# Retention in four chunks of 112 tokens and one of 128, where there were four of 128 and one of 64

## The chip, the cores and the metric

The kernel runs on one core of a Trainium2 chip. The metric is the device time of one execution in microseconds: 867.72 before the change, the median of three runs (867.5 to 868.18). A core has TensorE (PE, with its weight loads as PEld), VectorE (DVE), ScalarE (ACT), GpSimd (POOL) and SyncE (SP, which here only issues DMAs).

## The reference

Causal retention over 4 batches, 8 heads, 576 tokens and head dimension 64, and then two feed-forward layers over the 2304 x 512 result:

```python
scores = scale * np.matmul(q, k.transpose(0, 1, 3, 2))      # scale = 1/8
gamma = 1.0 - 2.0 ** (-5.0 - np.arange(H))
Dmat = np.where(rel >= 0, gamma[:, None, None] ** rel, 0.0)  # rel = row - column
ret = np.matmul(scores * Dmat, v)                            # 4 x 8 x 576 x 64
x = ret.transpose(0, 2, 1, 3).reshape(2304, 512)
h = x @ w_in;  x = np.maximum(0.01 * h, h) @ w_out           # 512 -> 2048 -> 512
h = x @ w2_in; out = (h - np.tanh(h)) @ w2_out
```

The weights of the layers arrive as 64-bit floats.

## The kernel before, in words

Retention is computed by chunks. For a chunk of tokens, the near part is the masked score matrix of the chunk with itself, times v. The far part is q, scaled by powers of gamma, times a state of 64 x 64 that sums k times v over all chunks before. Two heads make a pair, and there are 16 pairs (`order`). The first 64 partitions hold one head's dimensions and the other 64 the other's, so that two products of 64 rows (or with an output of 64 rows) lie side by side in the array. 576 tokens are four chunks of 128 (`MAIN` = 512) and a tail of 64.

One pair `i` goes through these steps. Each engine works through its own instructions in the order in which they are written:

- `load` (two pairs ahead, on SP): transposed q and k of the pair, and k and v by tokens. The v by tokens has a fifth chunk: the last 128 tokens.
- `prep_k` (ACT, L613): k by tokens times gamma to the power of minus the row, for the states. `prep_tail` (ACT, L621; for the first pair DVE, L623): copies the last 64 columns of q, not yet scaled, into a block-diagonal tile `bd`, whose other half was set to zero once.
- `scores` (PE, L632): for each chunk and head one product of 64 rows, 128 x 128. The two heads go to the two banks of `sc`.
- `prep_q` (POOL, L602 and L607): q times its powers of gamma in place, first the 512 columns, then the 64.
- `mask` (DVE, L646): scores times mask and decay table `cm_sb`, one instruction a head, into `pt`.
- `pair_steps`: for pairs from 5 on first `unit_h` (PE, L758) and `unit_o` (PE, L783), which are products of the first layer for tokens that are done. Then the outputs of pair `i - 1`: `outputs_far` (L697) for chunks 1 to 3 and `outputs_near` (L708) for chunks 0 to 3 into the bank `o`, and both again for the tail into `x_t`. Then for pair `i` `states_mm` (L665, into the bank `x_c`) and `scores_tail` (L638): one product over the whole array, of k of the last 128 tokens with `bd`, into `x_a`. `states` (L673 on ACT, three L675 on DVE) adds up the states. `finish` (L716, L717) writes the output of pair `i - 1` as a rounded part and a rest, the tail first. `mask_tail` (DVE, L655) masks the last scores on the late 64 partitions; the early 64 of that part of `pt` were set to zero once. At the end stand `prep_tail` and `prep_k` of pair `i + 1`.

`x_a` and `x_t` are parts of one bank, `x_e`. Waits between engines on PSUM are by bank: a reader of a bank waits for the writes to that bank that were written before it in the program, and the other way round.

Between these steps `fill` sets the work that turns weights into two-part operands: 64-bit words are loaded (L149), narrowed to 32 bits (ACT L166, DVE L172, L177, L183 twice) and split (ACT L255, POOL L256). `marks` says how many of these operations stand in which third of which pair; the first eight weight pieces are used in the units, the others are kept in DRAM for later. SP's order is that of the program. A `load` of pair `i + 2` waits for the buffer of pair `i - 1`.

An fp32 product shows as two matmul instructions. So "x16" of L632 is eight products.

After the stage, `layers` (L275, L309, L428 and their helpers) does the rest; the change does not touch it. Columns, rows and parts that the steps touch are in the listing.

Of the kernel before, what the change touches and what calls it, by code (L numbers as in the profile page):

```python
# [10 lines left out]
F32 = mybir.dt.float32  # L11
# [3 lines left out]
AF = mybir.ActivationFunctionType  # L15
ALU = mybir.AluOpType
PSUM = bass.MemoryType.PSUM

P = 128
CH = 128  # L20

# [14 lines left out]
def retention_moe_moe(  # L36
# [16 lines left out]
    nc = tc.nc  # L53
    B, NP, _, S = qT.shape
    NT, DM = out.shape
    NF = w1i.shape[0]
    KK = DM // P
    NFULL = S // CH
    TAIL = S - NFULL * CH
    NCH = NFULL + 1  # L60
    MAIN = NFULL * CH
    LATE = CH - TAIL
    GF = 4
# [491 lines left out]
    def retention():  # L555
        with ExitStack() as ac:
            ak = ac.enter_context(tc.tile_pool(name="ak", bufs=1))
            ap_ = ac.enter_context(tc.tile_pool(name="ap", bufs=3))
            cw_pool[0] = ac.enter_context(tc.tile_pool(name="c0", bufs=2))
            ps_s = ac.enter_context(tc.tile_pool(name="ps_s", bufs=1, space=PSUM))  # L560
            ps_a = ac.enter_context(tc.tile_pool(name="ps_a0", bufs=1, space=PSUM))

            x_e = ps_s.tile([P, 3, TAIL], F32, name="x_e")
            x_a, x_t = x_e[:, :2, :], x_e[:, 2, :]
            x_b = ps_s.tile([P, 2, QW], F32, name="x_b")
            x_c = ps_s.tile([P, 512], F32, name="x_c")
            c_ = x_c[:, :NFULL * 64].rearrange("p (c d) -> p c d", d=64)


            cm_sb = ak.tile([P, NP, 2, CH], F32, name="cm_sb")  # L570
            qt_sb = ak.tile([P, NP, CH], F32, name="qt_sb")
            kt_sb = ak.tile([P, NP, 2], F32, name="kt_sb")
            sts = [ak.tile([P, NFULL, 64], F32, name=f"st{i}") for i in range(2)]
            decay = ak.tile([P, NP], F32, name="decay")
            pt_ = [ak.tile([P, 2, S], F32, name=f"pt{i}") for i in range(2)]
            bds = [ak.tile([P, 2, TAIL], F32, name=f"bd{i}") for i in range(2)]
            qk, kv, pts = {}, {}, {}
            order = [(b, p) for b in range(B) for p in range(NP)]

            def load(i):  # L580
                load_qk(i)
                load_v(i)

            def load_qk(i):
# [4 lines left out]
                qk[i] = t  # L589

            def load_v(i):
                b, p = order[i]
                t = ap_.tile([P, NFULL + NCH, P], F32, tag="kv", name="kv")
                nc.sync.dma_start(out=t[:, :NFULL, :], in_=kn[b, p])
                nc.sync.dma_start(out=t[:, NFULL:, :], in_=vn[b, p])
                kv[i] = t

            def prep_q(i):

                b, p = order[i]  # L600
                q = qk[i][:, 1, :MAIN].rearrange("p (c r) -> p c r", r=CH)
                nc.gpsimd.tensor_tensor(  # L602
                    out=q, in0=q, in1=qt_sb[:, p:p + 1, :].to_broadcast([P, NFULL, CH]),
                    op=ALU.mult,
                )
                q = qk[i][:, 1, MAIN:]
                nc.gpsimd.tensor_tensor(out=q, in0=q, in1=qt_sb[:, p, :TAIL], op=ALU.mult)  # L607

            def prep_k(i):
                b, p = order[i]  # L610
                for h in range(2):
                    k = kv[i][:, :NFULL, 64 * h:64 * h + 64]
                    nc.scalar.activation(out=k, in_=k, func=AF.Copy, scale=kt_sb[:, p, h:h + 1])  # L613

            def prep_tail(i):

                q = qk[i][:, 1, MAIN:]
                for h in range(2):
                    o = slice(64 * h, 64 * h + 64)
                    if i:  # L620
                        nc.scalar.activation(out=bds[i % 2][o, h, :], in_=q[o], func=AF.Copy)  # L621
                    else:
                        nc.vector.tensor_copy(out=bds[i % 2][o, h, :], in_=q[o])  # L623

            def scores(i):
                kt, qt = qk[i][:, 0, :], qk[i][:, 1, :]
                sc = ps_s.tile([P, 2, 512], F32, tag="sc", name="sc")
                for c in range(NFULL):
                    cs = slice(c * CH, (c + 1) * CH)
                    for h in range(2):  # L630
                        r = slice(64 * h, 64 * h + 64)
                        nc.tensor.matmul(  # L632
                            out=sc[:, h, cs], lhsT=kt[r, cs], rhs=qt[r, cs], start=True, stop=True
                        )
                return sc

            def scores_tail(i):
                nc.tensor.matmul(  # L638
                    out=x_a, lhsT=qk[i][:, 0, S - CH:], rhs=bds[i % 2], start=True, stop=True
                )  # L640

            def mask(i, sc):
                b, p = order[i]
                pt = pt_[i % 2]
                for h in range(2):
                    nc.vector.tensor_tensor(  # L646
                        out=pt[:, h, :MAIN].rearrange("p (c r) -> p c r", r=CH),
                        in0=sc[:, h, :].rearrange("p (c r) -> p c r", r=CH),
                        in1=cm_sb[:, p, h:h + 1, :].to_broadcast([P, NFULL, CH]), op=ALU.mult,
                    )  # L650
                pts[i] = pt

            def mask_tail(i):
                b, p = order[i]
                nc.vector.tensor_tensor(  # L655
                    out=pts[i][LATE:, :, MAIN:], in0=x_a[LATE:], in1=cm_sb[LATE:, p, :, LATE:],
                    op=ALU.mult,
                )

            def states_mm(i):  # L660
                t = kv[i]
                for c in range(NFULL):
                    for h in range(2):
                        o = slice(64 * h, 64 * h + 64)
                        nc.tensor.matmul(  # L665
                            out=c_[o, c, :], lhsT=t[:, c, o], rhs=t[:, NFULL + c, o],
                            start=True, stop=True,
                        )
# [11 lines left out]
            def chunk_out(o_, c):  # L680
                n = min(CH, S - c * CH)
                cs = slice(c * CH, c * CH + n)
                return (o_[:, cs] if c < NFULL else x_t), cs
# [6 lines left out]
            def outputs_far(i, o_, chunks):  # L690

                q, st = qk[i][:, 1, :], sts[i % 2]
                for c in chunks:
                    dst, cs = chunk_out(o_, c)
                    for h in range(2):
                        o = slice(64 * h, 64 * h + 64)
                        nc.tensor.matmul(  # L697
                            out=dst[o], lhsT=st[o, c - 1, :], rhs=q[o, cs],
                            start=c in (1, NFULL), stop=False, skip_group_check=True,
                        )  # L700

            def outputs_near(i, o_, chunks):
                pt, t = pts[i], kv[i]
                for c in chunks:
                    dst, cs = chunk_out(o_, c)
                    for h in range(2):
                        o = slice(64 * h, 64 * h + 64)
                        nc.tensor.matmul(  # L708
                            out=dst[o], lhsT=t[:, NFULL + c, o], rhs=pt[:, h, cs],
                            start=False, stop=True, skip_group_check=True,  # L710
                        )
# [93 lines left out]
            def pair_steps(i, fast):  # L805
# [26 lines left out]
                if i + 1 < len(order):  # L832
                    prep_tail(i + 1)
                    prep_k(i + 1)

            t = ap_.tile([P, 2, S], F32, tag="qk", name="qk")
# [276 lines left out]
```

## Time and profile before

| | |
|---|---|
| median of 3 runs | 867.72 us |
| the profiled execution | 868.1 us, its span 866.1 us |
| mean granted TensorE clock | 0.998 |
| PE busy | 850.1 us (98%), 5728 instructions |
| DVE busy | 604.1 us (70%) |
| ACT busy | 451.2 us (52%) |
| POOL busy | 377.1 us (44%) |
| DMA | 134.43 MB, mean 155 GB/s |

The span is from the first to the last instruction; the device time holds 2.0 us more around it. Busy shares are means over stages with different limits. The chain of waits goes back from the last instruction, at each step to what released it. A line of it is a stretch of time on one engine. Matmuls are pipelined and their ends are modelled, so the start of the next line says more than the duration of one matmul.

### The profile page before, as it was taken

What the parts mean: (1) busy time and instruction counts of PE and PEld (TensorE: products, weight loads), DVE (VectorE), ACT (ScalarE), POOL (GpSimd) and SP (SyncE); (2) the same over time, 40 slices, a digit from 0 to 9 for tenths busy, and PEclk for the clock granted to TensorE, in tenths of its full rate; (3) what the DMA queues carried; (4) which work ended last, traced back from release to release, by engine and by line L of the source; (5) the groups of instructions that cost most, each with busy time, mean ns of one, the idle gap of its engine ahead of it and who ended that gap; (6) DMA issues with size and microseconds to landing.
All of it is one profiled execution on the core that took longest, in us unless ns stands there. A gap on an engine that the chain in (4) does not pass through costs nothing.

```text
span 866.1 us, 15237 instructions
## 1 busy us (share of the span) xinstructions
PE 850.1 (98%) x5728; PEld 748.2 (86%) x5728; DVE 604.1 (70%) x1038; ACT 451.2 (52%) x899; POOL 377.1 (44%) x304
## 2 busy tenths in 40 slices
PE   6999999999999999999999999999999999999997
PEld 5889999888888889888888898888999899999996
DVE  5995767587786676658765577756676667777675
ACT  4553444453255433454444577666556566566663
POOL 2541222040036302464365379655545445545553
PEclk9999999999999999999999999999999999999999
DMA  9835663433454533644444503572225412563112
GB/s 340 315 125 172 219 209 118 150 121 103 135 213 186 179 121 110 243 170 127 190 175 165 195 1 146 226 284 75 75 96 180 162 73 74 208 231 121 49 50 74
DMA packets 38778, 134.43 MB, mean 155 GB/s; under 512 B 4400, under 2 KB 5936, under 8 KB 36656
## 3 DMA queue, kind: packets, MB, share of 16 engines
q1 hardware_dynamic: 38272, 133.25, 43.7%
q8 instruction: 45, 0.74, 0.4%
q14 instruction: 29, 0.24, 0.1%
q10 hardware_dynamic: 432, 0.20, 0.1%
HBM read 97.26 MB, written 36.18 MB: 154 GB/s over the span
## 4 chain that ended last, share of the span: by engine, by line
PE 89%; DVE 4%; DMA 2%; issue 2%; POOL 1%; ACT 1%; POOLq 0%; ACTq 0%; SPq 0%; DVEq 0%
PE a L428 40%; PE h L275 22%; PE h L309 17%; PE a L783 3%; PE x_b L758 3%; PE o L708 1%; PE sc L632 1%; PE o L697 1%; DVE cw L183 1%; DMA acc<-in_w1i 1%; DMA cm_sb<-in_cmask 1%; DVE pt L646 1%; PE x_c L665 0%; DVE v L394 0%; DMA kt_sb<-in_ktab 0%
## 5 line engine op out<-in xcount | busy, mean ns | idle before, releaser
L428 PE MATMUL a<-w 128*128 128x512 f32 (+1 forms) x1680 | 395.2, 377 | 0.5 <-POOL w L400 0.5
L428 PEld LDWEIGHTS a<-w 128*128 128x128 f32 x1680 | 293.1, 188 | 48.9 <-POOL w L400 1.3
L256 POOL TENSOR_TENSOR w<-cw,w 128x512 fp32r<-128x512 f32 x80 | 113.5, 1436 | 233.6 <-ACT w L255 207.8
L275 PE MATMUL h<-xh,w 128*128 128x512 f32 (+1 forms) x672 | 187.1, 349 | 0.0
L368 POOL TENSOR_TENSOR v<-t,u 128x512 f32<-128x512 f32 (+1 forms) x76 | 93.1, 1225 | 100.5 <-ACT t L365 96.4
L275 PEld LDWEIGHTS h<-xh,w 128*128 128x128 f32 x672 | 119.5, 188 | 17.0
L400 POOL TENSOR_TENSOR w<-v,w 128x512 fp32r<-128x512 f32 (+1 forms) x76 | 96.1, 1265 | 63.9 <-ACT w L399 63.9
L354 ACT ACTIVATE w<-h 128x512 fp32r<-128x512 f32 (+1 forms) x68 | 37.2, 547 | 160.3 <-PE h L275 115.4
L275 PE MATMUL h<-xl,w 128*128 128x512 f32 (+1 forms) x336 | 117.0, 348 | 0.0
L309 PE MATMUL h<-xh,w 128*128 128x256 f32 x512 | 100.9, 281 | 0.2
L309 PEld LDWEIGHTS h<-xe,w 128*128 128x128 f32 x576 | 80.8, 189 | 10.7 <-DVE mk L303 3.1
L183 DVE SCALAR_TENSOR_TENSOR cw<-st,cw 128x512 uint32<-128x512 uint32 x96 | 86.4, 900 | 2.5
L394 DVE SCALAR_TENSOR_TENSOR v<-q,v 128x512 f32<-128x512 f32 (+1 forms) x76 | 60.8, 800 | 37.1 <-POOL v L368 37.1
L364 ACT ACTIVATE u<-h 128x512 f32<-128x512 f32 (+1 forms) x80 | 44.2, 553 | 80.4 <-DVE h L303 53.2
L309 PEld LDWEIGHTS h<-xh,w 128*128 128x128 f32 x512 | 83.1, 190 | 2.8 <-DVE v L397 1.5
L309 PE MATMUL h<-xe,w 128*128 128x256 f32 x576 | 84.3, 282 | 1.1 <-DVE mk L303 1.0
L505 DVE TENSOR_TENSOR acc<-a,acc 128x512 f32<-128x512 f32 (+1 forms) x114 | 72.1, 657 | 18.5 <-PE a L428 18.5
L399 ACT ACTIVATE w<-v 128x512 fp32r<-128x512 f32 (+1 forms) x76 | 45.3, 596 | 61.5 <-DVE v L397 59.0
L172 DVE TENSOR_SCALAR cw<-cw 128x512 f32<-128x512 f32 x64 | 33.1, 518 | 57.7 <-ACT cw L166 57.6
L309 PE MATMUL h<-xl,w 128*128 128x256 f32 x256 | 71.8, 281 | 0.0
L275 PEld LDWEIGHTS h<-xl,w 128*128 128x128 f32 x336 | 63.3, 188 | 8.6
L383 DVE TENSOR_TENSOR h<-h,t 128x512 f32<-128x512 f32 (+1 forms) x80 | 51.3, 641 | 15.2 <-ACT t L365 15.2
(82 smaller groups left out, 1159.8 us busy)
## 6 DMA issues: line engine op xcount, KB each, us to landing
kept<-w SPq DMA_DIRECT2D x48, 512.0 KB, 3.5
w<-kept SPq DMA_DIRECT2D x48, 512.0 KB, 4.8
xe<-xkept SPq DMA_DIRECT2D x12, 1536.0 KB, 6.7
st<-in_w2i SPq DMA_DIRECT2D x16, 512.0 KB, 3.5
st<-in_w1i SPq DMA_DIRECT2D x12, 512.0 KB, 4.1
st<-in_w1o SPq DMA_DIRECT2D x12, 512.0 KB, 3.5
xkept<-xe SPq DMA_DIRECT2D x4, 1536.0 KB, 6.7
kv<-in_vn SPq DMA_DIRECT2D x16, 320.0 KB, 5.2
```

The costliest lines, as they stand in the source:

```text
L183: nc.vector.scalar_tensor_tensor(out=t["w"], in0=t[src], scalar=scalar, in1=t["w"], op0=op, op1=ALU.bitwise_or)
L256: nc.gpsimd.tensor_tensor(out=wp[:, 1, :], in0=wf, in1=wp[:, 0, :].bitcast(F32), op=ALU.subtract)
L275: nc.tensor.matmul(out=ps[:, :n], lhsT=w[:, wi, cs], rhs=x[:, kk, t0:t0 + n], start=kk == 0 and i == 0, stop=kk == KK - 1 and i == 2,)
L309: nc.tensor.matmul(out=out_, lhsT=w[:, wi_, at:at + P], rhs=x(xi, kk), start=start and kk == 0 and j == 0, stop=stop and kk == 1 and j == ...
L364: nc.scalar.activation(out=u[:, :n], in_=h, func=AF.Square)
L368: nc.gpsimd.tensor_tensor(out=v[:, :n], in0=t_[:, :n], in1=u[:, :n], op=ALU.mult)
L383: nc.vector.tensor_tensor(out=h, in0=h, in1=tmp[s][1][:, :n], op=ALU.subtract)
L394: nc.vector.scalar_tensor_tensor(out=v, in0=q, scalar=RHO_A, in1=v, op0=ALU.add, op1=ALU.mult)
L399: nc.scalar.activation(out=gt[:, 0, g_at(s)], in_=v, func=AF.Copy)
L400: (nc.gpsimd if m else nc.vector).tensor_tensor(out=gt[:, 1, g_at(s)], in0=v, in1=gt[:, 0, g_at(s)].bitcast(F32), op=ALU.subtract)
L428: nc.tensor.matmul(out=o, lhsT=l, rhs=r, start=f == 0 and i == 0 and d % pack == 0, stop=f == GF - 1 and i == 2 and (d + 1) % pack == 0, s ...
L505: nc.vector.tensor_tensor(out=dst, in0=a, in1=dst, op=ALU.add)
```

## The change

The chunks are now four of 112 tokens (`MAIN` = 448) and a last one of 128. `chunks_of` gives both numbers. The last chunk's v is no longer a fifth chunk of the v by tokens; it lies behind k in the tile `qk` and comes with k's load (for the first pair by a DMA of its own, after its other four). The products, masks and tables of the chunks take 112 rows and columns, those of the last chunk 128.

The last scores are one product of 64 rows a head, straight from q, into two banks. The copies of q (`bd`) and the two constant zero areas go. As the last scores now read q itself, the scaling of its last 128 columns on POOL stands behind them in `pair_steps`. `x_e` has two banks: one holds the last scores of the first head and `x_t`, the other those of the second head and the states `c_`, which had the bank `x_c`.

```diff
-CH = 128
+def chunks_of(S):
+    n = -(-S // P) - 1
+    return n, (S - P) // n
...
-            x_e = ps_s.tile([P, 3, TAIL], F32, name="x_e")
-            x_a, x_t = x_e[:, :2, :], x_e[:, 2, :]
+            x_e = ps_s.tile([P, 2, 512], F32, name="x_e")
+            x_a, x_t = x_e[:, :, :P], x_e[:, 0, P:2 * P]
             x_b = ps_s.tile([P, 2, QW], F32, name="x_b")
-            x_c = ps_s.tile([P, 512], F32, name="x_c")
-            c_ = x_c[:, :NFULL * 64].rearrange("p (c d) -> p c d", d=64)
+            c_ = x_e[:, 1, P:P + NFULL * 64].rearrange("p (c d) -> p c d", d=64)
...
-            bds = [ak.tile([P, 2, TAIL], F32, name=f"bd{i}") for i in range(2)]
...
+            def qk_tile():
+                return ap_.tile([P, 2 * S + P], F32, tag="qk", name="qk")
...
+            def v_of(i, c, o):
+                if c < NFULL:
+                    return kv[i][:CH, NFULL + c, o]
+                return qk[i][:, 2 * S:][:, o]
...
-                nc.sync.dma_start(out=t[:, 1, :], in_=qT[b, p])
-                nc.sync.dma_start(out=t[:, 0, :], in_=kT[b, p])
+                nc.sync.dma_start(out=t[:, :S], in_=qT[b, p])
+                nc.sync.dma_start(out=t[:, S:], in_=kT[b, p])
...
-                t = ap_.tile([P, NFULL + NCH, P], F32, tag="kv", name="kv")
-                nc.sync.dma_start(out=t[:, :NFULL, :], in_=kn[b, p])
-                nc.sync.dma_start(out=t[:, NFULL:, :], in_=vn[b, p])
+                t = ap_.tile([P, 2 * NFULL, P], F32, tag="kv", name="kv")
+                nc.sync.dma_start(out=t[:CH, :NFULL, :], in_=kn[b, p])
+                nc.sync.dma_start(out=t[:CH, NFULL:, :], in_=vn[b, p])
...
-                q = qk[i][:, 1, MAIN:]
-                nc.gpsimd.tensor_tensor(out=q, in0=q, in1=qt_sb[:, p, :TAIL], op=ALU.mult)
+
+            def prep_tail(i):
+                b, p = order[i]
+                q = q_of(i, MAIN)
+                nc.gpsimd.tensor_tensor(out=q, in0=q, in1=qt_sb[:, p, :], op=ALU.mult)
...
-            def prep_tail(i):
-
-                q = qk[i][:, 1, MAIN:]
-                for h in range(2):
-                    o = slice(64 * h, 64 * h + 64)
-                    if i:
-                        nc.scalar.activation(out=bds[i % 2][o, h, :], in_=q[o], func=AF.Copy)
-                    else:
-                        nc.vector.tensor_copy(out=bds[i % 2][o, h, :], in_=q[o])
...
             def scores_tail(i):
-                nc.tensor.matmul(
-                    out=x_a, lhsT=qk[i][:, 0, S - CH:], rhs=bds[i % 2], start=True, stop=True
-                )
+                for h in range(2):
+                    r = slice(64 * h, 64 * h + 64)
+                    nc.tensor.matmul(
+                        out=x_a[:, h, :], lhsT=k_of(i, MAIN)[r], rhs=q_of(i, MAIN)[r],
+                        start=True, stop=True,
+                    )
...
-                    out=pts[i][LATE:, :, MAIN:], in0=x_a[LATE:], in1=cm_sb[LATE:, p, :, LATE:],
-                    op=ALU.mult,
+                    out=pts[i][:, :, MAIN:], in0=x_a, in1=cm_sb[:, p], op=ALU.mult,
...
                     states_mm(i)
                     scores_tail(i)
+                    prep_tail(i)
                     states(i)
...
                 if i + 1 < len(order):
-                    prep_tail(i + 1)
                     prep_k(i + 1)
 
-            t = ap_.tile([P, 2, S], F32, tag="qk", name="qk")
-            nc.sync.dma_start(out=t[:, 1, :], in_=qT[0, 0])
+            t = qk[0] = qk_tile()
+            nc.sync.dma_start(out=t[:, :S], in_=qT[0, 0])
             nc.scalar.dma_start(out=cm_sb[:, 0], in_=cmask[:, 0])
-            nc.sync.dma_start(out=t[:, 0, :], in_=kT[0, 0])
-            qk[0] = t
+            nc.sync.dma_start(out=t[:, S:2 * S], in_=kT[0, 0, :, :S])
             nc.scalar.dma_start(out=kt_sb, in_=ktab)
             nc.scalar.dma_start(out=qt_sb[:, 0, :], in_=qtab[:, 0, :])
             load_v(0)
+            nc.sync.dma_start(out=t[:, 2 * S:], in_=kT[0, 0, :, S:])
             load_qk(1)
...
-            for t in bds:
-                nc.vector.memset(t, 0.0)
-            for t in pt_:
-                nc.vector.memset(t[:LATE, :, MAIN:], 0.0)
...
-            prep_tail(0)
```

## Rows read from the trace of the kernel before

**Rows 1.** The page, chain that ended last: shares of the span by engine.

```profile
PE 89%; DVE 4%; DMA 2%; issue 2%; POOL 1%; ACT 1%; POOLq 0%; ACTq 0%; SPq 0%; DVEq 0%
```

**Rows 2.** Stretch, length; busy PE, PEld, DVE, ACT, POOL; clock, DMA share, GB/s.

```profile
18.00:30.00 12.00, 9.34 (x147) 7.58 (x142) 11.66 (x25) 7.92 (x23) 8.21 (x8) 1.00 1.04 374
...
64.90:150.00 85.10, 85.10 (x994) 77.94 (x995) 59.88 (x112) 36.59 (x89) 22.69 (x22) 1.00 0.55 178
...
150.00:866.10 716.10, 709.54 (x4038) 621.65 (x4037) 491.30 (x808) 380.17 (x726) 326.31 (x252) 1.00 0.40 143
```

**Rows 3.** The chain in order of time, the start: start us, us, what.

```profile
5.83 6.10 DMA acc<-in_w1i
...
11.95 5.97 DMA cm_sb<-in_cmask
...
18.01 1.29 DVE pt L646 x2
```

**Rows 4.** The chain in order of time, one steady pair, and the last unit.

```profile
96.47 0.80 PE o L697 x12
97.27 1.02 PE o L708 x16
98.29 0.26 PE x_e L697 x4
98.56 0.27 PE x_e L708 x4
98.82 0.47 PE x_c L665 x16
99.29 0.42 PE x_e L638 x2
99.70 1.09 PE sc L632 x16
100.80 2.94 PE x_b L758 x24
...
139.65 2.83 PE x_b L758 x24
```

**Rows 5.** Groups by line, 0 to 190 us: busy us, mean ns, idle before.

```profile
L646 DVE TENSOR_TENSOR pt<-sc,cm_sb 128x512 f32<-128x512 f32 x32 | 20.6, 686 | 6.1 <-DMA cm_sb<-in_cmask 3.1 <-PE sc L632 2.6
...
L655 DVE TENSOR_TENSOR pt<-x_e,cm_sb 64x128 f32<-64x128 f32 x16 | 4.7, 295 | 0.5
...
L717 DVE TENSOR_TENSOR xl<-o,xh 128x512 fp32r<-128x512 f32 x16 | 10.9, 680 | 0.3 <-ACT xh L716 0.3
...
L717 DVE TENSOR_TENSOR xl<-x_e,xh 128x64 fp32r<-128x64 f32 x16 | 3.5, 218 | 0.8 <-ACT xh L716 0.8
...
L602 POOL TENSOR_TENSOR qk<-qk,qt_sb 128x512 f32<-128x512 f32 x16 | 21.3, 1328 | 58.1 <-PE sc L632 30.5 <-issue 20.6 <-PE x_c L665 4.1
...
L607 POOL TENSOR_TENSOR qk<-qk,qt_sb 128x64 f32<-128x64 f32 x16 | 9.2, 577 | 0.0
```

**Rows 6.** Timeline, 46 to 52 us: start us, us, instruction, idle before and releaser.

```profile
46.98 1.40 DVE L183 SCALAR_TENSOR_TENSOR cw<-acc,cw 128x512 uint32<-128x512 uint32 x2
...
48.08 0.51 ACT L621 ACTIVATE bd<-qk 64x64 f32<-64x64 f32 x2
...
49.43 0.61 ACT L255 ACTIVATE w<-cw 128x512 fp32r<-128x512 f32 x1
...
50.12 1.28 POOL L256 TENSOR_TENSOR w<-cw,w 128x512 fp32r<-128x512 f32 x1 [4.41 <-ACT w L255]
...
51.46 0.50 PE L758 MATMUL x_b<-xh,w 128*128 128x256 f32 x2 [0.86 <-POOL w L256]
```

**Rows 7.** Timeline, DVE from 58 to 63 us.

```profile
58.86 0.91 DVE L675 SCALAR_TENSOR_TENSOR st<-st,decay,x_c 128x64 f32<-128x64 f32 x3 [0.89 <-ACT st L673]
...
60.86 1.92 DVE L183 SCALAR_TENSOR_TENSOR cw<-acc,cw 128x512 uint32<-128x512 uint32 x2
```

**Rows 8.** SP's own waits in the first 70 us: us, times, longest.

```profile
SPq L588 <- DMA cm_sb<-in_cmask: 1.4, 1, 1.4
```

More of the change, by code (lines that the diff above doesn't have):

```diff
@@ L57, in retention_moe_moe @@
     KK = DM // P
-    NFULL = S // CH
-    TAIL = S - NFULL * CH
-    NCH = NFULL + 1
+    NFULL, CH = chunks_of(S)
     MAIN = NFULL * CH
-    LATE = CH - TAIL
+    assert MAIN + P == S
     GF = 4
@@ L582, in load, with q_of, k_of @@
                 load_v(i)
+            def qk_tile():
+                return ap_.tile([P, 2 * S + P], F32, tag="qk", name="qk")
+            def q_of(i, lo=0, hi=S):
+                return qk[i][:, lo:hi]
+            def k_of(i, lo=0, hi=S):
+                return qk[i][:, S + lo:S + hi]
+            def v_of(i, c, o):
+                if c < NFULL:
+                    return kv[i][:CH, NFULL + c, o]
+                return qk[i][:, 2 * S:][:, o]
             def load_qk(i):
                 b, p = order[i]
-                t = ap_.tile([P, 2, S], F32, tag="qk", name="qk")
-                nc.sync.dma_start(out=t[:, 1, :], in_=qT[b, p])
-                nc.sync.dma_start(out=t[:, 0, :], in_=kT[b, p])
-                qk[i] = t
+                t = qk[i] = qk_tile()
+                nc.sync.dma_start(out=t[:, :S], in_=qT[b, p])
+                nc.sync.dma_start(out=t[:, S:], in_=kT[b, p])
             def load_v(i):
                 b, p = order[i]
-                t = ap_.tile([P, NFULL + NCH, P], F32, tag="kv", name="kv")
-                nc.sync.dma_start(out=t[:, :NFULL, :], in_=kn[b, p])
-                nc.sync.dma_start(out=t[:, NFULL:, :], in_=vn[b, p])
+                t = ap_.tile([P, 2 * NFULL, P], F32, tag="kv", name="kv")
+                nc.sync.dma_start(out=t[:CH, :NFULL, :], in_=kn[b, p])
+                nc.sync.dma_start(out=t[:CH, NFULL:, :], in_=vn[b, p])
                 kv[i] = t
@@ L600, in prep_q @@
                 b, p = order[i]
[L601 removed]
+                q = q_of(i, 0, MAIN).rearrange("p (c r) -> p c r", r=CH)
                 nc.gpsimd.tensor_tensor(
[L603 removed]
+                    out=q, in0=q, in1=qt_sb[:, p:p + 1, :CH].to_broadcast([P, NFULL, CH]),
                     op=ALU.mult,
                 )
[L606 to L607 removed]
+            def prep_tail(i):
+                b, p = order[i]
+                q = q_of(i, MAIN)
+                nc.gpsimd.tensor_tensor(out=q, in0=q, in1=qt_sb[:, p, :], op=ALU.mult)
             def prep_k(i):
@@ L611, in prep_k @@
                 for h in range(2):
-                    k = kv[i][:, :NFULL, 64 * h:64 * h + 64]
-                    nc.scalar.activation(out=k, in_=k, func=AF.Copy, scale=kt_sb[:, p, h:h + 1])
-            def prep_tail(i):
-                q = qk[i][:, 1, MAIN:]
-                for h in range(2):
-                    o = slice(64 * h, 64 * h + 64)
-                    if i:
-                        nc.scalar.activation(out=bds[i % 2][o, h, :], in_=q[o], func=AF.Copy)
-                    else:
-                        nc.vector.tensor_copy(out=bds[i % 2][o, h, :], in_=q[o])
+                    k = kv[i][:CH, :NFULL, 64 * h:64 * h + 64]
+                    nc.scalar.activation(out=k, in_=k, func=AF.Copy, scale=kt_sb[:CH, p, h:h + 1])
             def scores(i):
-                kt, qt = qk[i][:, 0, :], qk[i][:, 1, :]
+                kt, qt = k_of(i), q_of(i)
                 sc = ps_s.tile([P, 2, 512], F32, tag="sc", name="sc")
@@ L632, in scores @@
                         nc.tensor.matmul(
-                            out=sc[:, h, cs], lhsT=kt[r, cs], rhs=qt[r, cs], start=True, stop=True
+                            out=sc[:CH, h, cs], lhsT=kt[r, cs], rhs=qt[r, cs], start=True, stop=True
                         )
@@ L646, in mask @@
                     nc.vector.tensor_tensor(
-                        out=pt[:, h, :MAIN].rearrange("p (c r) -> p c r", r=CH),
-                        in0=sc[:, h, :].rearrange("p (c r) -> p c r", r=CH),
-                        in1=cm_sb[:, p, h:h + 1, :].to_broadcast([P, NFULL, CH]), op=ALU.mult,
+                        out=pt[:CH, h, :MAIN].rearrange("p (c r) -> p c r", r=CH),
+                        in0=sc[:CH, h, :MAIN].rearrange("p (c r) -> p c r", r=CH),
+                        in1=cm_sb[:CH, p, h:h + 1, :CH].to_broadcast([CH, NFULL, CH]),
+                        op=ALU.mult,
                     )
@@ L665, in states_mm @@
                         nc.tensor.matmul(
-                            out=c_[o, c, :], lhsT=t[:, c, o], rhs=t[:, NFULL + c, o],
+                            out=c_[o, c, :], lhsT=t[:CH, c, o], rhs=v_of(i, c, o),
                             start=True, stop=True,
@@ L680, in chunk_out @@
             def chunk_out(o_, c):
-                n = min(CH, S - c * CH)
-                cs = slice(c * CH, c * CH + n)
+                cs = slice(c * CH, S if c == NFULL else c * CH + CH)
                 return (o_[:, cs] if c < NFULL else x_t), cs
@@ L690, in outputs_far @@
             def outputs_far(i, o_, chunks):
-                q, st = qk[i][:, 1, :], sts[i % 2]
+                q, st = q_of(i), sts[i % 2]
                 for c in chunks:
@@ L702, in outputs_near @@
             def outputs_near(i, o_, chunks):
-                pt, t = pts[i], kv[i]
+                pt = pts[i]
                 for c in chunks:
@@ L708, in outputs_near @@
                         nc.tensor.matmul(
-                            out=dst[o], lhsT=t[:, NFULL + c, o], rhs=pt[:, h, cs],
+                            out=dst[o], lhsT=v_of(i, c, o),
+                            rhs=pt[:P if c == NFULL else CH, h, cs],
                             start=False, stop=True, skip_group_check=True,
@@ L1058 @@
     NP = H // 2
+    NFULL, CH = chunks_of(S)
     def heads_t(a):
@@ L1064, in tokens @@
         a = a.reshape(B, NP, 2, S, D).transpose(0, 1, 3, 2, 4).reshape(B, NP, S, 2 * D)
-        main = S // CH * CH
-        chunks = a[:, :, :main].reshape(B, NP, main // CH, CH, 2 * D)
         if last:
-            chunks = np.concatenate([chunks, a[:, :, None, S - CH:]], axis=2)
+            return a[:, :, S - P:]
+        chunks = a[:, :, :S - P].reshape(B, NP, NFULL, CH, 2 * D)
         return np.ascontiguousarray(chunks.transpose(0, 1, 3, 2, 4))
@@ L1084 @@
     scale = 1.0 / np.sqrt(D)
-    r = np.arange(CH)
+    r = np.arange(P)
     rel = r[None, :] - r[:, None]
@@ L1090 @@
     consts = {
-        "cmask": mask.reshape(NP, 2, CH, CH).transpose(2, 0, 1, 3),
+        "cmask": mask.reshape(NP, 2, P, P).transpose(2, 0, 1, 3),
         "qtab": row_gamma[:, :, None] ** (CH + r) * scale,
-        "ktab": back.reshape(CH, NP, 2),
+        "ktab": back.reshape(P, NP, 2),
     }
     arrays = {
-        "qT": heads_t(q), "kT": heads_t(k), "kn": tokens(k, False), "vn": tokens(v, True),
+        "qT": heads_t(q), "kT": np.concatenate([heads_t(k), tokens(v, True)], axis=3),
+        "kn": tokens(k, False), "vn": tokens(v, False),
         "w1i": w_in(inputs["moe_w_in"]), "w1o": w_out(inputs["moe_w_out"]),
```

5 lines of the change are left out of this document (2 added, 3 removed).

## The prediction

> **What bounds the kernel now.** I read the chain of work that ended last first, then a table of busy times by stretch, then the chain again in order of time, and the timeline where the chain leaves TensorE. The chain's shares say that TensorE carries 89% of the span and VectorE 4% [rows 1]. The reader should see next that this holds by stage: from 18 to 30 us VectorE works 11.66 of 12 us while the DMA engines are full (share 1.04, 374 GB/s); from 64.9 to 150 us TensorE is busy for all 85.1 us, VectorE for 59.9; after 150 us it is layer work that the change does not touch, 99% TensorE [rows 2]. [...] The change lives in the retention stage, which ends at about 148 us; a microsecond won on its chain is won at the end.
>
> Three pieces of that stage set the time. To 18 us it is DMA: weight piece 0 needs 6.1 us to land, and only its landing lets the third head pair's mask table be issued, which takes 5.97 us more and releases VectorE at 18.01 [rows 3]. Then VectorE, and from about 46 to 65 us a mixture of ScalarE, GpSimd and VectorE making weight pieces. From 65 us on TensorE is without a gap.
>
> **The change part by part: TensorE.** Each line of the chain of one steady head pair is a run of products in one division of the array (the forms 64\*64, 128\*64 and so on) [rows 4]. A head's output of 128 columns takes four runs of 128 for L708 (1.02 us) and one of 64 in the tail (0.27 us): (1.02 - 0.27) / (512 - 64) = 1.67 ns a column. L697 gives (0.80 - 0.26) / (384 - 64) = 1.69. What stays at zero columns is 0.27 - 0.107 = 0.163 and 0.26 - 0.108 = 0.152 us: the price of entering another division. L665 follows the tail of L708 in the same division and has 0.47 - 256 x 1.67 = 0.04. L638 (one product over the whole array, 128 columns) has 0.42 - 0.214 = 0.206, and L632 after it 1.09 - 0.855 = 0.235.
>
> After the change, with 112 columns a chunk and 128 in the tail:
> - L697 main: 0.152 + 3 x 112 x 1.67 = 0.71 for 0.80; L708 main: 0.163 + 448 x 1.67 = 0.91 for 1.02. Their tails: 0.152 + 0.214 = 0.37 and 0.163 + 0.214 = 0.38 for 0.26 and 0.27. Together +0.03 us a pair. The states product keeps its 64 columns: nothing.
> - Last scores: two products of 64 rows in two PSUM banks, side by side as the two heads in L632 are, so still 128 columns, entry 0.22 (between 0.206 and 0.235): 0.43. The scores of the next pair follow in the same division: 0.04 + 448 x 1.67 = 0.79. Together 1.22 for 0.42 + 1.09 = 1.51: -0.29 us. Bounds: -0.11 if the second entry stays, -0.34 if nothing is left of it.
>
> From 65 us to the end of the stage there are seven such tail-and-scores pairs and nine outputs, and the last tail is now followed by a layer product in another division (2.94 us where it enters from L632, 2.83 where it enters from L638: +0.11) [rows 4]. Sum: 7 x -0.29 + 9 x 0.03 + 0.11 = -1.65 us; bounds -0.4 and -2.0. All of it is on the path, as TensorE has no gap there.
>
> **VectorE and GpSimd.** The masks lose 2 x 64 columns at the slope of the two L717 rows, (680 - 218) / 448 = 1.03 ns: -0.13 us; the tail mask goes from 128 to 256 elements a partition, +0.13; the two L717 trade 64 columns [rows 5]. VectorE, the bound of 18 to 45 us, gets nothing. GpSimd's scaling of q trades 64 columns between L602 and L607 [rows 5]. L607 is moved from right behind L602 to behind the last scores. It now waits for TensorE; behind it on GpSimd stand the weight splits of the pair's third filling, which wait for ScalarE work issued later anyway. Its reader, the far tail output of the next pair, comes several us later. I take 0; were that cover gone, it costs its duration, 0.58 us, once a pair in which GpSimd is late.
>
> **ScalarE.** Two copies of q, 0.51 us a pair, go. From 65 us on that is worth nothing. At 49 us it is on the path: VectorE has finished the weight piece at 46.98 + 1.40 = 48.38, but ScalarE does L621 and L613 first and reaches L255 at 49.43; GpSimd follows at 50.12, and TensorE resumes at 51.46 after 0.86 us without work [rows 6]. Without L621, and with one tail-and-scores saved ahead of it, L255 starts some 0.7 us earlier (at most 1.05, by VectorE). Against it stands an added wait: the states c_ now share a bank with one head's last scores, so the first state copy waits for these too, by about L638's 0.42 us, and VectorE's three state steps stand behind it. Where VectorE is late this is covered. In the pair at 58.6 us it is not: L675 there had already waited 0.89 us, and L183 behind it makes the piece for which TensorE stops at 64 us [rows 7]. That gives back 0.4, less what L183 (1.92 us for two there, 1.40 at 47 us) wins when L607 no longer runs beside it: 0 to 0.5, I take 0.25. Sum of this part -0.45, bounds 0 and -1.05.
>
> **The start.** A pair's loads were 288 + 288 + 256 + 320 = 1152 KB and are 288 + 352 + 224 + 224 = 1088. Three pairs lie ahead of the mask table of 18 us: 192 KB at 374 GB/s [rows 2] is 0.53 us. But the first pair now has one DMA more. The ninth issue, L588, waited 1.4 us for one of the first to land [rows 8]; now the second pair's q is that ninth. Full queues hide this; if they run dry it costs up to 1.4 us. I take -0.4, near the row that shows the queues full; bounds -0.55 and +1.4.
>
> [...]
>
> **Sum.** -1.65 - 0.45 - 0.4 = -2.5 us. The profiled execution took 868.1 us (span 866.1 and 2.0 around it), so 865.6; it lies 0.4 above the median of 867.72, so against that 865.2 us.
>
> **Rivals.**
> - The second entry is not saved, or the two small last products get in each other's way: what speaks for it is that the row of L632 shows 0.235 at its entry, not which part of it is the division. TensorE then gains 0.4: 867.72 - 0.4 - 0.85 = 866.5 us.
> - The queues run dry at the start: +1.4 for -0.4 gives 867.0. For it: the wait of rows 8. Against it: full queues in rows 2.
> [...]
> - Both stalls at 50 and 64 us go, nothing is given back and nothing of the second entry is left: -2.0 - 1.05 - 0.5 gives 864.2.
> - The other side: two heads' products no longer run side by side when their operands have 112 rows or columns. Every product in the trace has 64 or 128 of each, so the trace can't exclude it. If all is lost, scores and L708 pay 448 x 1.67 = 0.75 us each more a pair, 1.5 us over eight pairs, +12: about 877. The point from which it decides is a loss of a fifth (8 x 0.3 = 2.5 us). Against it: 64\*64, 128\*64 and 64\*128 all show the same 1.67 to 1.69.
>
> **How the numbers follow.** Forecast 0.42; 112-partition loads at full price 0.12; entry not saved 0.20; dry queues 0.10; both stalls gone 0.09; products no longer side by side 0.07. The predicted time is 865.2. The forecast's own range is 864.4 to 866.1. With the second rival's 866.5 and the third's 867.0, and the bounds of the start and of the entry, the range for 8 in 10 is 863.9 to 867.6; above it lies the last rival, below it little. 0.2%, what a measurement of this kernel can tell from no change, is 1.74 us: faster is below 865.98. Forecast (nine tenths of it), the 112-partition case and the stalls case are faster, with a tenth of the rest: 0.38 + 0.10 + 0.09 + 0.01 = 0.58. Slower takes the last rival and an unlucky sum of entry and dry queues, 0.10. The rest, 0.32, is no change.
>
> **What would show each step.** In the chain of a steady pair: L697 and L708 main at 0.71 and 0.91, tails at 0.37 and 0.38, last scores 0.43, next scores 0.79, and a pair period of 9.98 us shorter by about 0.26. Scores still near 1.0 mean the entry stayed; L708 well above 0.91 means 112 rows cost. In the timeline: the first mask of the third pair at about 17.6 us, L255 near 48.7, and the stall after 50 us gone or halved. The stage's end should move from 148 to about 145.5, and the layers after it should be as long as before. The prediction is wrong if the stage's gain is lost in the layers, or if the start moves later by a microsecond.

## The result, and the profile after

The changed kernel is slower: 878.24 us, the median of four runs (877.87 to 879.02), against 867.93 (867.50 to 868.18) for the kernel before on the same chip. The ratio is 1.0121 [1.0103, 1.0138], 10.3 us. The forecast was 2.5 us faster. The profiled execution after has a span of 875.9 us; before it was 866.1. One run of e8, below, was slow (1404.57 us at a granted clock of 0.656) and is left out of its median.

The part that the prediction worked out with most care came out as forecast. The chain in order of time, of after: start us, us, what. It holds one steady pair, the unit that follows the last tail, and the end of the stage.

```profile
96.95 0.72 PE o L705 x12
97.67 0.92 PE o L716 x16
98.59 0.37 PE x_e L705 x4
98.95 0.37 PE x_e L716 x4
99.32 0.47 PE x_e L674 x16
99.79 0.42 PE x_e L646 x4
100.21 0.78 PE sc L638 x16
101.00 2.93 PE x_b L767 x24
103.93 2.72 PE a L792 x24
106.65 0.72 PE o L705 x12
...
149.71 2.94 PE x_b L767 x24
...
160.76 4.09 PE h L277 x36
```

L705, L716, L674, L646, L638 and L767 are L697, L708, L665, L638, L632 and L758 of [rows 4]. The pair takes 106.65 - 96.95 = 9.70 us for 9.98. The near and far products, both tails, the last scores (0.42 for a forecast of 0.43) and the next scores (0.78 for 0.79) all stand where they were put.

And yet the stage ends 10 us later. The same mark in the kernel before, the first long run of layer products, from its chain in order of time:

```profile
150.68 4.10 PE h L275 x36
```

160.76 against 150.68: +10.08. From that mark to the end both kernels take the same, 715.1 us after and 715.4 before. So the layers have no part in it. The loss is ahead of it; busy times by stretch, of after (stretch, length; busy PE, PEld, DVE, ACT, POOL; clock, DMA share, GB/s):

```profile
18.00:30.00 12.00, 8.87 (x124) 7.16 (x122) 9.59 (x22) 3.33 (x9) 5.22 (x5) 0.86 1.02 309
...
51.40:64.90 13.50, 10.15 (x87) 9.42 (x84) 11.08 (x19) 5.47 (x12) 5.38 (x4) 0.75 0.26 84
75.30:160.80 85.50, 84.94 (x1016) 77.27 (x1017) 58.92 (x112) 32.98 (x75) 22.06 (x23) 1.00 0.55 172
160.80:875.90 715.10, 708.99 (x4032) 620.96 (x4030) 491.45 (x808) 380.55 (x726) 326.19 (x252) 1.00 0.40 143
```

From 18 to 30 us VectorE, the bound of that stretch in [rows 2], now works 9.59 of 12 us for 11.66, so it waits more. ScalarE does 3.33 for 7.92. The DMA engines are as full as before (1.02 for 1.04) but move 309 GB/s for 374. Between 51.4 and 64.9 us TensorE works 10.15 of 13.5 us, and its granted clock is 0.75. In the kernel before, TensorE's last stop for a weight piece ends at 64.86, in this one at 75.27, 10.4 us later: the whole loss has been made by then.

The second of the following rows names the first cause. ScalarE's waits to 160 us, of after (who waits, on what: us, times, longest):

```profile
ACT st L682 <- PE x_e L646: 37.3, 14, 5.2
ACT xh L725 <- DVE st L684: 19.8, 15, 2.3
```

The same view of before, the lines of the same two instructions:

```profile
ACT st L673 <- PE x_c L665: 28.3, 12, 4.8
ACT xh L716 <- PE x_e L638: 1.9, 10, 0.2
```

The first wait is long in both, and it is not the loss: in e5 below, which is faster than the kernel before, it is 41.0 us. L725 is `finish` on ScalarE: it rounds the tail outputs `x_t` of pair i - 1. In 15 pairs it waits for VectorE's state steps of pair i, 19.8 us in all. Nothing in the mathematics asks for that: `x_t` has nothing to do with the states. But both lie in the one tile `x_e` now, `x_t` in its first bank and the states `c_` in its second. The program has the state steps (readers of `c_`) ahead of `finish` (a reader of `x_t`). The description of the kernel before said that waits on PSUM go by bank, and that a reader waits for writes. Here a reader of one bank waits for readers of another; e4 and e6 below test that.

What follows from it is seen in the timeline of after, 52 to 60 us (start us, us, instruction, idle before and releaser):

```profile
52.84 0.22 ACT L682 ACTIVATE st<-x_e 128x64 f32<-128x64 f32 x1 [0.52 <-PE x_e L646]
...
53.24 0.68 DVE L174 TENSOR_SCALAR cw<-cw 128x512 f32<-128x512 f32 x1
...
53.84 0.68 DVE L812 COPY acc<-a 128x512 f32<-128x512 f32 x1
...
54.44 0.90 DVE L684 SCALAR_TENSOR_TENSOR st<-st,decay,x_e 128x64 f32<-128x64 f32 x3
...
55.37 0.28 ACT L725 ACTIVATE xh<-x_e 128x128 fp32r<-128x128 f32 x1 [2.31 <-DVE st L684]
55.55 0.54 ACT L725 ACTIVATE xh<-o 128x448 fp32r<-128x448 f32 x1
...
55.97 0.90 ACT L629 ACTIVATE kv<-kv,kt_sb 112x256 f32<-112x256 f32 x2
...
56.77 0.62 ACT L257 ACTIVATE w<-cw 128x512 fp32r<-128x512 f32 x1
...
57.45 0.58 PE L767 MATMUL x_b<-xh,w 128*128 128x256 f32 x1 [2.29 <-ACT w L257]
57.47 1.78 POOL L258 TENSOR_TENSOR w<-cw,w 128x512 fp32r<-128x512 f32 x1 [3.83 <-DVE cw L179]
...
59.31 0.80 PE L767 MATMUL x_b<-xh,w 128*128 128x256 f32 x2 [1.06 <-POOL w L258]
```

ScalarE copies the first state at 52.84 and is then idle for 2.31 us, until VectorE, which had weight work (L174) and a copy (L812) in front of the steps, has done them at 55.34. Behind `finish` on ScalarE stand `prep_k` (L629) and the weight split L257. L257 ends at 57.39. GpSimd had been idle for 3.83 us when its half, L258, started at 57.47; its row names VectorE's L179, which ends at 57.41, 0.02 us after L257. TensorE stood still for 2.29 us and again for 1.06.

Its clock is down by then. The granted clock of the stretch is 0.75; in shorter stretches it is 0.50 from 57.45 to 61.80 us, right behind the stop of 2.29 us, and 1.00 again from 64.90. The ten matmuls of `x_b` that start at 59.31 take 2.50 us in the chain, where ten take 1.45 at a granted clock of 1.00. From there to the next outputs (65.66) it is 6.35 us; the same work took 4.27 before (51.46 to 55.73). So, as an estimate from these two lengths, some 2 us of the loss are paid through the clock in this execution.

VectorE's and GpSimd's groups, which answer to [rows 5] (0 to 190 us: busy us, mean ns, idle before):

```profile
L655 DVE TENSOR_TENSOR pt<-sc,cm_sb 112x448 f32<-112x448 f32 x32 | 18.4, 616 | 8.4 <-PE sc L638 5.9 <-DMA cm_sb<-in_cmask 2.3
L726 DVE TENSOR_TENSOR xl<-o,xh 128x448 fp32r<-128x448 f32 x16 | 10.0, 625 | 2.3
L665 DVE TENSOR_TENSOR pt<-x_e,cm_sb 128x256 f32<-128x256 f32 x16 | 6.6, 415 | 0.0
L726 DVE TENSOR_TENSOR xl<-x_e,xh 128x128 fp32r<-128x128 f32 x16 | 4.7, 292 | 6.0 <-ACT xh L725 6.0
```

The durations are the forecast's (the masks 616 ns for 686, the tail mask 415 for 295). New is the idle time of the last group: 6.0 us on ScalarE, for 0.8 before.

The start came later where it was to come earlier. The chain in order of time, the start of after:

```profile
6.88 5.92 DMA acc<-in_w1i
12.82 7.20 DMA cm_sb<-in_cmask
20.11 1.16 DVE pt L655 x2
```

The third pair's mask starts at 20.11 for 18.01 [rows 3]. SP's own waits to 70 us still have the one wait of [rows 8], now of the second pair's q:

```profile
SPq L601 <- DMA cm_sb<-in_cmask: 1.7, 1, 1.7
```

### The profile page after: what moved, and what is told of

Read it like the earlier page. It is cut to its first block, busy times and chain, and to the rows that moved or that the text cites. A ratio compares the mean times of both kernels' runs of the same rounds, so it can differ in the third digit from the quotient of the medians.

```text
span 875.9 us, 15250 instructions
## 1 busy us (share of the span) xinstructions
PE 854.0 (97%) x5760; PEld 750.4 (86%) x5760; DVE 602.1 (69%) x1032; ACT 443.9 (51%) x869; POOL 375.5 (43%) x304
## 4 chain that ended last, share of the span: by engine, by line
PE 89%; DVE 3%; DMA 3%; issue 1%; ACT 1%; POOL 1%; ACTq 0%; POOLq 0%; SPq 0%; DVEq 0%
PE a L430 39%; PE h L277 21%; PE h L311 17%; PE a L792 4%; PE x_b L767 3%; PE o L716 1%; PE o L705 1%; DMA cm_sb<-in_cmask 1%; DMA acc<-in_w1i 1%; PE sc L638 1%; DMA qt_sb<-in_qtab 1%; PE x_e L674 1%; PE x_e L716 1%; PE x_e L705 1%; PE x_e L646 1%
## 5 line engine op out<-in xcount | busy, mean ns | idle before, releaser
L258 POOL TENSOR_TENSOR w<-cw,w 128x512 fp32r<-128x512 f32 x80 | 114.0, 1441 | 239.7 <-ACT w L257 205.7
L185 DVE SCALAR_TENSOR_TENSOR cw<-st,cw 128x512 uint32<-128x512 uint32 x96 | 86.5, 901 | 2.5
L174 DVE TENSOR_SCALAR cw<-cw 128x512 f32<-128x512 f32 x64 | 33.1, 517 | 56.6 <-ACT cw L168 56.6
```

The source lines that it names most:

```text
L185: nc.vector.scalar_tensor_tensor(out=t["w"], in0=t[src], scalar=scalar, in1=t["w"], op0=op, op1=ALU.bitwise_or)
L258: nc.gpsimd.tensor_tensor(out=wp[:, 1, :], in0=wf, in1=wp[:, 0, :].bitcast(F32), op=ALU.subtract)
```

## The experiments

Three causes were in question: the wait of one reader of `x_e` for another; slower loads of `kn` and `vn`, which now go to 112 partitions; and the ninth DMA. Each run was timed against the kernel before on its own chip (medians 868.1 for e1 to e4 and 868.19 for e5 to e8); runs on different chips are compared by their ratios to it.

**e1_order.** The changed kernel; ScalarE's first state copy, then the tail's `finish`, then VectorE's state steps.

```diff
...
-                    states(i)
+                    states_first(i)
                 if i:
                     finish(i - 1, x_t, MAIN, S)
+                if i < len(order):
+                    states(i)
+                if i:
                     finish(i - 1, ot[:, :MAIN], 0, MAIN)
```

> The changed kernel with one reordering: ScalarE writes its first state copy, then the tail of the last pair's output, and only then come VectorE's three state steps. Wait theory (the tail's output lies in the same PSUM tile as the states, so ScalarE's rounding of it waits for VectorE's state steps, and everything behind it on ScalarE waits too): ScalarE's waits for the state steps (11.4 us in seven waits up to 80 us) vanish, TensorE's stops before 76 us shrink, 878.2 falls by 4 to 7 us to 871-874. Load theory (the loads of 112 partitions or of longer rows move fewer bytes a microsecond): no change of the time beyond 1 us, 877-878.5; the third pair's mask still starts at about 20.1 us.

Measured: 869.39 us, ratio 1.0018 [1.0005, 1.0031]. The order of three instructions gives back 8.9 of the 10.3 us, more than expected. ScalarE's wait for VectorE's state steps is gone from its view altogether. It is VectorE that waits now, for `finish` on ScalarE (L728 for L727: 7.7 us of idle time to 100 us), and that costs little. What is left is 1.3 us over the kernel before.

**e2_pad.** The changed kernel; `kn` and `vn` are loaded on 128 partitions: the rows of a chunk and the 16 tokens behind it, which nothing reads.

```diff
-                nc.sync.dma_start(out=t[:CH, :NFULL, :], in_=kn[b, p])
-                nc.sync.dma_start(out=t[:CH, NFULL:, :], in_=vn[b, p])
+                nc.sync.dma_start(out=t[:, :NFULL, :], in_=kn[b, p])
+                nc.sync.dma_start(out=t[:, NFULL:, :], in_=vn[b, p])
...
```

> The changed kernel with k and v by tokens loaded on all 128 partitions (rows 112 to 127 of a chunk are the next tokens and are not used), 256 KB in place of 224 a load. Load theory, by partitions: the third pair's mask starts near 18 us instead of 20.1 although more bytes are moved, the DMA engines move about 375 GB/s again, and the time falls by 2 to 4 us to 874-876. Load theory, by the longer rows of k with v behind it (2816 bytes for 2304): no gain, or 0.3 us lost by the bytes. Wait theory alone: no change, 877.5-878.5.

Measured: 876.93 us, 1.0109 [1.0091, 1.0127]. That lies between the two theories' ranges. 1.3 us of the loss went, but the intervals of the two kernels overlap, and the third pair's mask, expected near 18 us, starts at 21.09 (in an execution of 879.98 us, the slowest of the four). So it is a miss for the theory of loads. That the wait on ScalarE hides the loads is a reading; what speaks for it is that the same edit wins 1.6 us once that wait is gone (e3 against e1).

**e3_both.** Both edits.

> Both edits together. If the two theories together hold the whole loss: TensorE's gain of the forecast is left, 865 to 867 us. If a third cause is open: above 868.

Measured: 867.79 us, 0.9994 [0.9984, 1.0003]: no difference from before. It lies between what was expected of two causes (865 to 867) and of a third one (above 868); at the upper end, so a third cause was looked for.

**e4_before_shared.** The kernel before, with nothing changed but the place of the states: they move into the second bank of the tile that holds `x_t`. Products, loads and order are those of before; both halves of the added wait come with it.

```diff
-            x_e = ps_s.tile([P, 3, TAIL], F32, name="x_e")
-            x_a, x_t = x_e[:, :2, :], x_e[:, 2, :]
+            x_e = ps_s.tile([P, 2, 512], F32, name="x_e")
+            x_a = x_e[:, 0, :2 * TAIL].rearrange("p (h r) -> p h r", h=2)
+            x_t = x_e[:, 0, 2 * TAIL:3 * TAIL]
...
-            c_ = x_c[:, :NFULL * 64].rearrange("p (c d) -> p c d", d=64)
+            c_ = x_e[:, 1, :NFULL * 64].rearrange("p (c d) -> p c d", d=64)
```

> The kernel before, with one part of the change alone: the states move from a PSUM tile of their own into the second bank of the tile that holds the tail's output and the last scores (now two banks). Products, copies and loads are as before. Wait theory: ScalarE waits for VectorE's state steps as in the changed kernel, and the time rises by 2.5 to 6 us to 870.5-874. Load theory: 868, no change.

Measured: 878.34 us, 1.0120 [1.0105, 1.0135], +10.2 us: the whole loss in one move of a tile, far more than the 2.5 to 6 that were expected. ScalarE's waits to 160 us, of this kernel:

```profile
ACT xh L716 <- DVE st L675: 20.6, 15, 2.6
```

It is the row of after, in number of waits and in size. No instruction of this kernel touches both banks of the tile, so the bank can't be what the wait goes by. The granted clock from 51.4 to 64.9 us, where the changed kernel had 0.75, is 1.00 here (stretch, length; busy PE, PEld, DVE, ACT, POOL; clock, DMA share, GB/s):

```profile
51.40:64.90 13.50, 11.06 (x132) 9.81 (x130) 12.07 (x20) 6.84 (x15) 5.35 (x5) 1.00 0.28 89
```

From 30 to 51.4 us it is 0.92. So as much is lost without a fall of the clock in the stretch that was shown. The third pair's mask is late here too (20.29 us) with loads that were not touched, so a late third mask does not by itself speak of slow loads.

**e5_tail_late.** e3, and the first pair's last v, the DMA that was added, is issued behind the second pair's loads.

```diff
             load_v(0)
-            nc.sync.dma_start(out=t[:, 2 * S:], in_=kT[0, 0, :, S:])
             load_qk(1)
             load_v(1)
+            nc.sync.dma_start(out=t[:, 2 * S:], in_=kT[0, 0, :, S:])
```

> Both edits, and the first pair's DMA of the last v moved behind the second pair's loads, so that the second pair's q is again the eighth DMA. Dry-queue theory (with one DMA more ahead of it, the second pair's q waits for a landing, and the queues run dry at 6 to 7.5 us, 133 to 240 GB/s there): that hole closes, the third pair's mask starts at 18 to 19 us instead of 21.4, and 867.8 falls to 865-866.5. If VectorE or TensorE cover the start anyway: 867.5-868.

Measured: 866.04 us, 0.9974 [0.9965, 0.9982]: faster than the kernel before by 2.15 us, and faster than e3 by some 1.75 (e3 has 0.9994 [0.9984, 1.0003]). This is the fastest version. DMA engines from 0 to 20 us in 40 slices, GB/s, of e3:

```profile
GB/s 0 0 0 60 113 238 394 385 356 371 395 374 217 133 210 238 340 352 326 336 335 381 406 385 384 404 397 415 385 408 410 379 380 299 201 176 345 144 73 340
```

The same of e5:

```profile
GB/s 0 0 0 99 136 260 357 390 331 328 335 382 374 391 413 412 365 371 400 401 399 358 379 397 398 382 391 402 401 434 368 337 367 392 402 383 397 402 406 387
```

e3 has a hole from 6 to 8 us (217, 133, 210, 238) and another from 17 to 19.5 us; e5 has none. SP's issues to 20 us, of e3:

```profile
2.60 0.43 SPq L857 DMA_DIRECT2D qk<-in_kT  x1
4.47 0.33 SPq L601 DMA_DIRECT2D qk<-in_qT  x1
```

and of e5:

```profile
2.60 0.43 SPq L601 DMA_DIRECT2D qk<-in_qT  x1
4.45 0.33 SPq L602 DMA_DIRECT2D qk<-in_kT  x1
```

The issue at 2.60 us is the last before SP stops for some 1.4 us. In e3 the small load takes that place, and everything behind it is one place later: the second pair's q is issued at 4.47 for 2.60.

**e6_two_tiles.** e5's loads, the order of the change as it was, and the same two banks as two tiles of one bank (the tail's mask is then two instructions).

```diff
-            x_e = ps_s.tile([P, 2, 512], F32, name="x_e")
-            x_a, x_t = x_e[:, :, :P], x_e[:, 0, P:2 * P]
+            x_e = [ps_s.tile([P, 512], F32, name=f"x_e{h}") for h in range(2)]
+            x_t = x_e[0][:, P:2 * P]
...
-            c_ = x_e[:, 1, P:P + NFULL * 64].rearrange("p (c d) -> p c d", d=64)
+            c_ = x_e[1][:, P:P + NFULL * 64].rearrange("p (c d) -> p c d", d=64)
```

> The order of the changed kernel (state steps ahead of the tail's output), but the two banks are two tiles, one with one head's last scores and the tail's output, one with the other head's and the states; the tail's mask is then two VectorE instructions, some 0.15 us a pair more. Loads on 128 partitions, the last v late. If the wait comes from the common tile: within 0.7 us of the run with the late last v, 865-867. If it comes from the order or from the banks: ScalarE waits for the state steps again and the time is above 872.

Measured: 866.49 us, 0.9978 [0.9968, 0.9987], as e5 by its interval. The order and the places in the two banks are those of the change, and ScalarE's wait for the state steps is gone from its view. So it belonged to the tile, not to a bank.

**e7_before_ninth.** The kernel before; the first pair's v is loaded by two DMAs in place of one, so that the second pair's q is the ninth.

```diff
-            load_v(0)
+            t = kv[0] = ap_.tile([P, NFULL + NCH, P], F32, tag="kv", name="kv")
+            nc.sync.dma_start(out=t[:, :NFULL, :], in_=kn[0, 0])
+            nc.sync.dma_start(out=t[:, NFULL:2 * NFULL, :], in_=vn[0, 0, :, :NFULL])
+            nc.sync.dma_start(out=t[:, 2 * NFULL:, :], in_=vn[0, 0, :, NFULL:])
```

> The kernel before, with the first pair's load of v cut in two DMAs (four chunks, and the fifth), so that the second pair's q is the ninth DMA. Dry-queue theory: the second pair's q is issued at 4.5 instead of 2.6 us, a hole of one to two microseconds appears in the DMA traffic, and the time rises by 0.7 to 2 us to 868.8-870. If the start is covered: 868.1, no change.

Measured: 869.19 us, 1.0007 [0.9998, 1.0016]: inconclusive. The median is inside the 868.8 to 870 that were expected, but the interval has no change in it too, and at most 1.4 us. SP issued that q at 4.71 us for 2.60, and the third pair's mask started at 20.18 for 18.01. In the profiled execution, which with 870.08 us is one of the longest of the eleven, this delay is not made up: the first layer product starts at 152.57 us for 150.68.

**e8_order_late.** e1 and the late last v; the loads on 112 partitions stay. It differs from e5 in these loads alone.

> The reordering and the late last v, but the loads of k and v by tokens on 112 partitions as in the changed kernel. Against the run with 128 partitions it prices these loads without the hole. Load theory by partitions: 0.7 to 2.5 us slower than that run, 866.5-868.5. If only the hole cost: the same as that run.

Measured: 869.78 us, 1.0015 [1.0006, 1.0024], against 866.04 for e5 on the same chip: the loads on 112 partitions cost 3.7 us, with 64 KB a pair less to move. That is more than the 866.5 to 868.5 that were expected. DMA from 0 to 20 us, of e8:

```profile
DMA packets 3408, 5.75 MB, mean 288 GB/s; under 512 B 509, under 2 KB 1405, under 8 KB 3407
...
q1 hardware_dynamic: 2975, 5.53, 90.6%
```

and of e5:

```profile
DMA packets 3838, 6.76 MB, mean 338 GB/s; under 512 B 544, under 2 KB 1441, under 8 KB 3837
...
q1 hardware_dynamic: 3405, 6.55, 89.7%
```

The engines of queue q1 are as busy (90.6 and 89.7%) and move 5.53 MB for 6.55. In the mean of all packets of the queue that is 0.906 x 16 x 20 us / 2975 = 97 ns against 0.897 x 320 / 3405 = 84 ns. These means mix loads of all kinds. By size, in the same traces and the same 20 us: packets of 2048 bytes, which are those of `kn` and `vn` alone, last 116 ns in the mean in e8 and 88 in e5; those of 4096 bytes, the weights, whose loads were not touched, last 218 and 166. In the traces of after and of before, over the same 20 us, packets of 2048 bytes last 118.3 and 86.5 ns (in before those of `kn` alone, as its `vn` has 2560 bytes), and those of 4096 bytes 208.0 and 163.5. So what runs beside these loads slows down too. As e5 keeps the longer rows of k, these are not the reason.

## Why the prediction was wrong, step by step

**TensorE: right, in mechanism and size.** A steady pair is 0.28 us shorter for a forecast 0.26. The marks are the end of TensorE's last stop for a weight piece and the first long run of layer products (the "148" of the prediction is the start of the last unit; by this mark the stage of before ends at 150.68). The chain of before, and of after:

```profile
64.86 1.45 PE a L783 x10
```

```profile
75.27 1.44 PE a L792 x10
```

Of e5:

```profile
51.21 1.45 PE x_b L769 x10
...
64.60 1.45 PE a L794 x10
...
148.93 4.09 PE h L277 x36
```

Of e6:

```profile
50.88 1.42 PE x_b L768 x10
...
64.05 1.40 PE a L793 x10
```

In e5 the stretch takes 148.93 - 64.60 = 84.33 us; before, it took 150.68 - 64.86 = 85.82. That is -1.49 for -1.65; e6, with its end mark at 147.98, has -1.89. In the changed kernel itself the same stretch takes 160.76 - 75.27 = 85.49, and most of the gain is lost: the chain leaves TensorE in two pairs for ScalarE and VectorE's state steps.

**The failed step: the added wait.** The prediction had it half: "the states c_ now share a bank with one head's last scores, so the first state copy waits for these too". It priced that at 0.42 us and stopped there. It asked who writes where a reader reads, and not who else reads. The tile with the states also holds the tail outputs `x_t`, their reader on ScalarE stands behind VectorE's readers of `c_` in the program, and so ScalarE waits for VectorE: 19.8 us in 15 pairs. Before 65 us, where VectorE has weight work ahead of its state steps, this reaches the weight splits behind `finish` and stops TensorE. e4 puts the states into that tile and changes nothing else, both halves of the wait with it, and pays 10.2 us. e1 takes away only the half that the prediction did not see, ScalarE's wait for the state steps, and gets 8.9 back; e6 takes it away in another way.

The wait goes further than a shared bank: `x_t` and `c_` are in different banks, the wait came all the same (19.8 us in 15 waits in after, 20.6 in 15 in e4), and it went when the two banks became two tiles (e6).

**ScalarE's two copies: right in sign by one run, the size open.** In e5 TensorE resumes at 51.21 us for 51.46 [rows 6], still after 0.86 us without work, and at 64.60 for 64.86: -0.26 for -0.45. But there the third pair's mask starts at 17.68 us for 18.01, so an earlier start can account for all of it. In e6 that mask starts at 18.01, as before; L258, GpSimd's half of the weight split (L256 of before), which follows ScalarE's, starts at 49.55 for 50.12 (-0.57; the forecast had ScalarE's half some 0.7 earlier), and TensorE resumes at 50.88 and 64.05, -0.58 and -0.81. The stalls stayed in both.

**The start: wrong in sign.** The -0.4 was chosen "near the row that shows the queues full". Two things that had a chance in the forecast were real, and the first was weighed far too low: 112-partition loads at full price, at 0.12, and dry queues, at 0.10. No row or run up to the prediction shows what a load of 112 partitions costs, so the 0.12 was the author's estimate. The runs show that such loads cost more than those on 128, by 3.7 us (e8 against e5): the bytes saved win nothing, and a packet of `kn` or `vn` takes 116 ns where it was 88. The ninth DMA left the holes that the rival of dry queues described, and its price, 1.75 us from e3 to e5, is near that rival's 1.8 (+1.4 for -0.4); in the kernel before the same shift costs no more than 1.4 (e7). With the loads on 112 partitions, as in the change, taking it back won nothing that can be told from the noise (1.0018 in e1, 1.0015 in e8), so for the changed kernel itself no price of the ninth DMA is shown.

**VectorE, GpSimd and the two heads side by side: right.** The durations of VectorE are as forecast, GpSimd's scaling of the tail of q, which was moved, stands in the chain of after once, at 52.88 us, with 4.06 us of waiting for the weight piece behind it, so it delayed nothing there, and products of 112 rows or columns run as those of 128 (0.92 us for L716, for a forecast 0.91 that was worked out from products of 128). The rival at 877 us landed near the time that was measured, but by a mechanism that the rows exclude: that was luck.

With the three causes taken out, e5 has 866.04 for 868.19: -0.26% [-0.35, -0.18], or -2.15 us. Its loads are as large as before, so the forecast's sum without the start, -1.65 - 0.45 = -2.1, is the one to compare. That the two agree to 0.05 us is in part chance: the spans of the profiled executions (864.0 and 866.1) differ by -0.26 up to the end of the last stop for a weight piece, -1.49 behind it and -0.35 in the layers, which the change doesn't touch, and e6 has -1.7 us. The losses do not add up one by one: e1's 8.9, the loads' 1.3 (e2), 1.6 (e1 to e3) or 3.7 (e8 to e5), and the small load's 1.75 (e3 to e5) or nothing (e1 to e8). That whichever is latest at the start covers the others would explain this; no run shows it by itself.

Left open: why packets take longer when loads go to 112 partitions. No run here changed the number of partitions alone to anything but 112 and 128.

## What to carry to other kernels

When two buffers are put into one tile, list every reader and writer of each in program order and look at the pairs across engines, readers with readers too; a move that saves nothing and costs nothing in instructions was worth 10 us here. If they must share, order the program so that an engine with a queue of urgent work behind it comes first. And at the start of a program count DMAs and partitions, not only bytes: here loads of 112 rows were slower than the same loads padded to 128, by 3.7 us (e8 against e5).

## What the runs showed of the hardware

With `kn` and `vn` loaded to 112 partitions their packets of 2048 bytes lasted 116 ns in the mean, and 88 with loads to 128; the packets of the weights beside them lasted 218 and 166 ns, with DMA engines equally busy (0 to 20 us, e8 and e5). Padding these loads with rows that nobody reads won 3.7 us (e5 against e8). The last scores take 0.42 us in the chain as one product over the whole array and as two products of 64 rows side by side. Products with 112 columns cost (0.92 - 0.37) / (448 - 128) = 1.72 ns a column in L716 of after, for 1.67 with 128 columns before. After TensorE had stood still for 2.29 us its granted clock was 0.50 from 57.45 to 61.80 us, and ten matmuls took 2.50 us for 1.45 (after).
